# Moving the head that is scored alone ahead of the last pair, in a fused attention and GeGLU kernel

## The chip, the cores and the metric

The kernel runs on one core of one Trainium2 chip, in one launch. The metric is the device time of that launch in microseconds (us). Three runs of the kernel before took 1405.23, 1408.26 and 1406.68 us; their median is 1406.68 us.

## The reference, cut to what matters

One transformer block in float32: S = 2048 rows, D = 512, 32 query heads of 16 columns that share one key head and one value head, F = 1792.

```
q = layernorm(x) @ wq ; k = layernorm(x) @ wk ; v = layernorm(x) @ wv
h = x + softmax(q k^T / 4) v @ wo                     # 32 heads over one k and one v
h2 = h + (gelu(layernorm(h) @ w_gate) * (layernorm(h) @ w_up)) @ w_down
```

## The kernel before, in words

**Attention.** The 2048 query rows are four blocks of 512, the 32 heads eight groups of four, and the keys sixteen stretches of 128. One block, group and stretch is a *chunk*: 4 x 8 x 16 = 512 chunks, numbered here from 0 in the order of the work, so that chunk 128 begins the second block. For a chunk TensorE (PE) forms scores of two *pairs* of heads; a pair is two matmuls that run side by side in the upper and the lower 64 rows of the array (`scores`, L369 to L376, through `score_head`, L380). ScalarE (ACT) takes the exponential of a pair at once, 128x1024 (L376), into a tile `p`. Four matmuls then *weigh* the values with the four heads of the chunk (`weigh`, L386), summing in the PSUM bank `acc` over the sixteen chunks of a group; after the last of them VectorE (DVE) copies the sums out (`evacuate`, the copy `oT<-acc` at L399), and SyncE's queue (SP) sends them to memory and fetches them back turned. Two PSUM buffers of two banks hold the scores of a pair (`pss`), so a pair's scores wait for the exponential of the pair two before it.

**Dense products.** The output projection (`pp`), the gate and up projections (`pg`, `pu`) and the down projection (`pd`) of an earlier block are woven into the attention of the next. Each weight is split in a high and a low part, so a product is a list of terms. A product's upper 64 rows of the contraction are its *first* row and its lower 64 rows its *second*; `step` issues one matmul of a first row and one of a second row, six steps behind (`LAG`), and the two run side by side. Three PSUM banks serve these rows in turn (`take_bank`, from the front of the list `spare`); a bank is put back when its row has ended, and the next row in it waits for DVE's copy or add out of it (L623 and L626 for `pp`, L698 and L702 for `pg` and `pu`, L765 for `pd`). Other DVE work of a product stands in the list `later`, two entries of which `side(2)` issues at each row's end and at each cycle's start.

**The order of the work** is written out by hand. From pair 280 the main loop runs in cycles: `finish(RUN)` weighs four chunks in one run, then a string of moves is played, in which `s` scores a pair, `d` is a step, `2` and `1` score one head alone. A head alone fills one half of the array and a row of a dense product the other. `1` scores the second head of the next pair at the very end of a cycle, into a dense bank, and `2` its first head at the start of the next; so the strings are `2` + WOVEN after a cycle that ended with such a half, and FRESH after one that did not. ACT takes each of the two halves apart (128x512, L1089). A cycle in which the queue of dense products has too little ready is a PAUSE: single chunks, weighed and scored with no step. Pauses stand at chunks 244 to 247 and 372 to 379.

In what follows a *slot* is one place in PE's order that two matmuls share: a pair's two heads, a first and a second row, or half a pair and one row. A woven cycle is a run of four chunks and 26 slots: eight for scores (seven pairs, and the two halves) and eighteen for dense products, counting those beside the halves.

**The opening** of the dense work is the stretch from chunk 134 to chunk 152: the lead-in ends with six pairs in a row, five chunks are weighed in one run, and the four projections `pp_0_0` to `pp_0_3` of the first block follow. Each ends in a layer norm on DVE and GpSimd (POOL), and PE turns its result with four transposes (`pxt`, L636, `turn`), which DVE splits into `x2h` and `x2l` (L641, L642); `pg` starts when the last of the four is split. In the later blocks three of the four turns are DVE transposes of 32x32 blocks instead (`xt<-xb`, L657, `turn_blocks`).

A tanh (ACT, L714) is issued at a cycle's start (`bend`); its products on DVE (`gate`: L720, L723, then L732, L736) were put into `later` after the run of weighings had been issued.

Of the kernel before, what the change touches and what calls it, by code (L numbers as in the profile page):

```python
# [13 lines left out]
AF = mybir.ActivationFunctionType  # L14
# [41 lines left out]

AHEAD = {240: 3, 248: 2}

BOUND_CYCLES = (6, 8)

HOLD = -4

# [3 lines left out]
def kernel(  # L66
# [97 lines left out]
    def run(outer, first):  # L164
# [204 lines left out]
        def scores(i, p, qg, kc, u):  # L369

            third = width == 1 and (2 * i + u) % 3 == 2
            pool, tag, bufs = (ps, "s3", 1) if third else (pss, "s", 2)
            s = pool.tile([P, 2, T], F32, tag=tag, bufs=bufs, name=f"s_{i}_{u}")
            for a in range(2):
                score_head(s[:, a, :], qg, kc, u, a)
            nc.scalar.activation(p[:, 2 * u : 2 * u + 2, :], s, AF.Exp, scale=SCALE)  # L376

        def score_head(s, qg, kc, u, a):
            rows = slice(64 * a, 64 * a + KR)
            nc.tensor.matmul(  # L380
                s, kaug[rows, kc * P : (kc + 1) * P], qg[rows, u, :], start=True, stop=True
            )
# [201 lines left out]
        def side(n):  # L584
            while later and n > 0:
                later.pop(0)()
                n -= 1
# [468 lines left out]
        def open_pair(n):  # L1056

            nonlocal acc
            i, u = divmod(n, 2)
            b, r = divmod(i, PER)  # L1060
            g, kc = divmod(r, KC)
            if u == 0:
                if kc == 0:
                    cur["qg"] = qgs.pop((b, g))
                    acc = psa.tile([P, T], F32, tag="acc", bufs=1, name=f"acc_{b}_{g}")
                if kc == 2 and b * NG + g + 1 < NB * NG:
                    key = divmod(b * NG + g + 1, NG)
                    qgs[key] = load_q(*key)
                cur["p"] = sb.tile([P, 4, T], F32, tag="p", bufs=PB, name=f"p_{i}")
            return i, u, b, g, kc  # L1070

        def score(n):
            i, u, b, g, kc = open_pair(n)
            scores(i, cur["p"], cur["qg"], kc, u)
            if u == 1:
                pend.append((b, g, kc, cur["p"], acc, n))

        def score_half(n, a):
            if a == 1:
                cur["open"] = open_pair(n)  # L1080
            i, u, b, g, kc = cur["open"]
# [6 lines left out]
            score_head(s, cur["qg"], kc, u, a)  # L1088
            nc.scalar.activation(cur["p"][:, 2 * u + a, :], s, AF.Exp, scale=SCALE)  # L1089

        banks.close()
        psa = outer.enter_context(
# [6 lines left out]
        width = 1  # L1099


        n, lead = 0, 2 * PER + 24
        with tc.manual_schedule(engines={mybir.EngineType.SP, mybir.EngineType.DVE}):
            parts = None
            if first:
                work = later_q()
                parts = part_weights(early.enter_context(tc.tile_pool(name="parts", bufs=1)))


            normed = True  # L1110
# [12 lines left out]
            def norm():  # L1123
                nonlocal normed
                if not normed:
                    next(work)
                    normed = True

            def pace():
                nonlocal n, parts, db, tiny  # L1130
                if n == 2 * PER:
                    drain()
                    for _ in parts or ():
                        pass
# [12 lines left out]
                if n == 2 * PER + 8:  # L1147
                    prime()

            moves = {"s": pace, "p": visit, "n": norm, "v": partial(finish, 1)}  # L1150
            for move in OPENING + PERIOD * (PER // KC):
                moves[move]()
            while n < lead:
                pace()
                if n > lead - 6:
                    finish(len(pend) - RUN)
                elif n % 4 == 2 and len(pend) > 2:
                    finish(1)
                elif n % 4 == 0:
                    finish(len(pend) - 2)  # L1160
# [34 lines left out]
        def urgent():  # L1195
            i = at - 1 if left[0] else at
            return i < len(queue) and queue[i][0].startswith("pp") and any(
                queue[j][0].startswith("pg") for j in range(i, min(i + TB + 1, len(queue)))
            )

        def turns_left():
            return scaled_at and all(
# [1 line left out]
                for b, _ in scaled_at  # L1204
            )

        odd, cycle = False, 0
        while pend:
            if first and cycle in BOUND_CYCLES:
                bound_flag(BOUND_CYCLES.index(cycle))  # L1210
            cycle += 1
            last = n >= end - 2 * RUN
            steps = WOVEN.count("d") + 1
            want = 12 if urgent() else steps * AHEAD.get(n % (2 * PER), 1)
            idle = n == end or available() < (want if n < end - 2 * PER // 8 else steps)
            if idle and (n == end or urgent()):
                while available():
                    step()
            if idle and not available() and (
                at == len(queue) or queue[at - 1][0].startswith("pp")  # L1220
            ):
# [5 lines left out]
            idle = idle and not behind and available() < want  # L1227
            finish(1 if idle else RUN)
            clock += 4 if idle else 4 * RUN
            if behind:  # L1230
                for b_t in list(scaled_at):
                    del scaled_at[b_t]
                    turn(*b_t)
            for key in bent:
                later.extend(gate(*key))
            side(2 * len(bent))
            if idle:
                moves = "2" * odd + PAUSE[odd:]
            else:
                part = not last and not scaled_at  # L1240
                moves = ("2" + WOVEN if odd else FRESH) + "d1"[part]
            for move in moves:
                if move == "d":
                    if available():
                        step()
                elif move == "v":
                    finish(1)
                    clock += 4
                elif move == "1":
                    if clock - freed.get(spare[0], -EMPTY) < EMPTY or not available():  # L1250
                        if available():
                            step()
                        odd = False
                    else:
                        score_half(n, 1)
                        step(second=False)
                        odd = True
                elif move == "2":
                    score_half(n, 0)
                    if ahead > LAG:  # L1260
                        step(first=False)
                    n, odd = n + 1, False
                elif n < end:
                    score(n)
                    n += 1
                    clock += 1
        assert not odd
        while available():
            step()
# [386 lines left out]
```

## Time and profile before

| what | value |
|---|---|
| median of three runs | 1406.68 us |
| the profiled execution | 1408.69 us |
| its span, first to last instruction | 1406.9 us |
| mean granted TensorE clock | 0.996 |
| PE busy | 1383.1 us (98%) |
| ACT busy | 1035.2 us (74%) |
| DVE busy | 657.5 us (47%) |

The profiled execution is 1.8 us longer than its span and 2.0 us longer than the median of the three runs. A busy PE is not a PE at its peak: matmuls overlap by the model of their ends, so small waits between them do not show as idle time. They show as spacing between the starts of matmuls, and as waits of PEld, the part of PE that loads weights ahead of a matmul.

### The profile page before, as it was taken

How to read it: one execution, taken by the hardware profiler on the slowest of the kernel's cores; microseconds unless marked ns; L12 is line 12 of the kernel's file. 1: busy time of each engine (PE TensorE's matmuls, PEld its weight loads, DVE VectorE, ACT ScalarE, POOL GpSimd, SP SyncE). 2: the span in 40 equal slices, each digit the busy share in tenths (PEclk: the TensorE clock that was granted, in tenths of full speed). 3: DMA queues.
4: the chain of work that ended last, by engine and by line, in shares of the span. 5: the costliest groups of instructions: out<-in, count | busy, mean ns of one | idle time of the engine just before them, and what ended most of it. 6: DMA issues, size and time to landing. Idle time of an engine off the chain costs nothing.

```text
span 1406.9 us, 25386 instructions
## 1 busy us (share of the span) xinstructions
PE 1383.1 (98%) x10406; PEld 758.4 (54%) x10406; DVE 657.5 (47%) x1097; ACT 1035.2 (74%) x1241; POOL 239.5 (17%) x346
## 2 busy tenths in 40 slices
PE   9999999999999999999999999999999999999998
PEld 7533333325555555545555555545555555558886
DVE  7413131313364453547364453537455353546665
ACT  8899999986687877877787777787778777772000
POOL 7576777621000000001000000001100000002000
PEclk9999999999999999999999999999999999999999
DMA  4566776753222423311432333311333332333552
GB/s 162 165 214 194 236 236 231 221 175 112 80 92 71 138 96 118 102 57 43 157 110 87 132 91 114 102 58 35 136 105 116 102 103 82 123 115 125 192 205 95
DMA packets 66784, 180.32 MB, mean 128 GB/s; under 512 B 9672, under 2 KB 9672, under 8 KB 66628
## 3 DMA queue, kind: packets, MB, share of 16 engines
q1 hardware_dynamic: 55324, 143.29, 31.0%
q0 software_dynamic: 10208, 35.26, 7.6%
q8 instruction: 84, 1.38, 0.4%
q14 instruction: 40, 0.33, 0.1%
q10 hardware_dynamic: 1128, 0.07, 0.1%
HBM read 130.87 MB, written 47.45 MB: 127 GB/s over the span
## 4 chain that ended last, share of the span: by engine, by line
PE 89%; ACT 5%; DVE 3%; DMA 2%; issue 1%; POOL 0%; SPq 0%; ACTq 0%; POOLq 0%
PE acc L386 32%; PE s L380 19%; PE pg L836 8%; PE pu L836 8%; PE pd L836 7%; ACT p L376 5%; PE pq L225 3%; PE pd L874 3%; PE pg L874 3%; PE pu L874 3%; PE pp L836 1%; PE pp L938 1%; DMA w<-w_d 1%; DMA x<-in_A_x_dram 1%; DVE xt L657 1%
## 5 line engine op out<-in xcount | busy, mean ns | idle before, releaser
L376 ACT ACTIVATE p<-s 128x1024 f32<-128x1024 f32 x940 | 878.5, 1050 | 40.7 <-PE s L380 37.9
L386 PE MATMUL acc<-p,v_sb 128*32 128x512 f32 x4096 | 481.9, 599 | 0.0
L380 PE MATMUL s<-qg,kaug 50*128 50x512 f32 x1984 | 421.5, 426 | 9.2 <-ACT p L376 7.3
L380 PEld LDWEIGHTS s<-qg,kaug 50*128 50x128 f32 x1984 | 184.7, 184 | 272.4 <-ACT p L376 141.3
L386 PEld LDWEIGHTS acc<-p,v_sb 128*32 128x32 f32 x4096 | 113.1, 109 | 253.2 <-issue 241.4
L1089 ACT ACTIVATE p<-s 128x512 f32<-128x512 f32 x168 | 106.0, 631 | 190.7 <-PE s L380 150.8
L836 PE MATMUL pg<-x2h,w 64*128 64x512 f32 x672 | 209.7, 401 | 1.4 <-DVE g L702 0.7
L836 PE MATMUL pu<-x2h,w 64*128 64x512 f32 x672 | 208.4, 398 | 0.4 <-DMA w<-w_d 0.4
L836 PE MATMUL pd<-w,gh 64*128 64x512 f32 x624 | 115.5, 394 | 1.9 <-DVE gh L732 1.1
L143 POOL TENSOR_SCALAR rstd<-mv 128x1 f32<-128x1 f32 x16 | 3.6, 223 | 668.2 <-DVE mv L141 668.0
L836 PEld LDWEIGHTS pg<-x2h,w 64*128 64x128 f32 x672 | 99.1, 187 | 10.7 <-DVE g L702 2.1
L765 DVE TENSOR_TENSOR h<-h,pd 128x512 f32<-128x512 f32 x80 | 54.9, 686 | 104.5 <-PE pd L836 79.8
L836 PEld LDWEIGHTS pu<-x2h,w 64*128 64x128 f32 x672 | 97.7, 186 | 7.2 <-issue 0.7
L836 PE MATMUL pg<-x2l,w 64*128 64x512 f32 x336 | 101.3, 395 | 0.2 <-DVE x2l L642 0.2
L836 PE MATMUL pu<-x2l,w 64*128 64x512 f32 x336 | 99.9, 392 | 0.0
L399 DVE COPY oT<-acc 128x512 f32<-128x512 f32 x32 | 22.1, 691 | 146.0 <-PE acc L386 145.8
L836 PE MATMUL pd<-w,gl 64*128 64x512 f32 x312 | 81.1, 400 | 0.0
L836 PEld LDWEIGHTS pd<-w,gh 64*128 64x128 f32 x624 | 69.7, 187 | 11.5 <-DVE gh L732 1.5
L992 ACT ACTIVATE ga<-ga 128x512 f32<-128x512 f32 x14 | 8.8, 632 | 88.5 <-DVE ga L989 88.5
L702 DVE TENSOR_TENSOR u<-u,pu 128x512 f32<-128x512 f32 x42 | 28.8, 685 | 85.2 <-PE pu L836 56.4
L422 DVE RECIPROCAL oc<-oc 128x128 f32<-128x128 f32 x64 | 56.6, 920 | 17.7 <-DMA oc<-acc_d 13.8
L702 DVE TENSOR_TENSOR g<-g,pg 128x512 f32<-128x512 f32 x42 | 28.8, 687 | 67.7 <-PE pg L836 52.2
(256 smaller groups left out, 1538.6 us busy)
## 6 DMA issues: line engine op xcount, KB each, us to landing
w<-w_d SPq DMA_DIRECT2D x126, 512.0 KB
w<-w_d SPq DMA_DIRECT2D x21, 1024.0 KB
qg<-q_d SPq DMA_DIRECT2D x62, 200.0 KB
q_d<-qh SPq DMA_DIRECT2D x32, 256.0 KB
acc_d<-oT SPq DMA_DIRECT2D x31, 256.0 KB
oc<-acc_d SPq DMA_DIRECT2D x124, 64.0 KB
w_d<-w_0b POOLq DMA_DIRECT2D x14, 512.0 KB, 4.2
w_d<-w_1b POOLq DMA_DIRECT2D x14, 512.0 KB, 3.8
```

The source lines that it names most:

```text
L225: nc.tensor.matmul(pq, wt[c][:, d, :], xt[:, d, :], start=(n == 0), stop=(n == 3 * DC - 1),)
L376: nc.scalar.activation(p[:, 2 * u : 2 * u + 2, :], s, AF.Exp, scale=SCALE)
L380: nc.tensor.matmul(s, kaug[rows, kc * P : (kc + 1) * P], qg[rows, u, :], start=True, stop=True)
L386: nc.tensor.matmul(acc[32 * j : 32 * j + 32, :], v_sb[:, kc, :], p[:, j, :], start=(kc == 0), stop=(kc == KC - 1), skip_group_check=True,)
L399: nc.vector.tensor_copy(oT, acc)
L422: nc.vector.reciprocal(oc[:, 1, sl], oc[:, 1, sl])
L657: nc.vector.transpose(raw[32 * k : 32 * k + 32, :, 32 * i : 32 * i + 32], x[32 * i : 32 * i + 32, :, k, :],)
L702: nc.vector.tensor_tensor(half, half, bank, op=ALU.add)
L765: nc.vector.tensor_tensor(hs[b, t], hs[b, t], bank, op=ALU.add)
L836: nc.tensor.matmul(bank, lhsT[r], rhs[r], start=(k == 0), stop=(k == n - 1), skip_group_check=True,)
L874: nc.tensor.matmul(bank, lhsT, rhs, start=(i == 0), stop=(i == len(ts) - 1))
L1089: nc.scalar.activation(cur["p"][:, 2 * u + a, :], s, AF.Exp, scale=SCALE)
```

## The change

Four things change; the diff below is cut to them.

- `1` moves from behind the last `s` to before it, in WOVEN and FRESH: the lone head of pair n+1 is scored before pair n, and its exponential is issued to ACT before that of pair n. `open_pair` now hands over all that belongs to a pair, so that pair n+1 can be opened before pair n is scored. EMPTY, the age in ticks that a dense bank must have before a lone head may use it, goes from 6 to 5, and the move now stands one tick earlier. No lone head is scored while a projection `pp` is among the last two products begun (`projecting`).
- The opening gets lists of its own (CYCLES): twice, cycles that weigh three, three and two chunks. Where the queue has too little ready, a list's plain string weighs and scores single chunks. The lead-in ends one pair earlier (279).
- A run of four weighs three chunks, then issues the first two of a waiting tanh's products to DVE, and only then weighs the fourth, behind which the copy of the sums is issued.
- The rule for when a cycle pauses is rewritten: `urgent` is gone, and the reserve (RESERVE) holds for all blocks but the last.

```diff
+CYCLES = (
+    (3, "ssdddddsdddsddds", "vssvssvs"),
+    (3, "ssdddddsdddsddds", "vssvssvs"),
+    (2, "ssdddddsdddsdddsddds", "ssvssvss"),
+)
+OPENING_LISTS = 2
-WOVEN = "sdddsdddsdddsdddsdddsdds"
-FRESH = "ssdddddsdddsdddsdddsddsds"
+WOVEN = "2sdddsdddsdddsdddsdddsdd1s"
+FRESH = "ssdddddsdddsdddsdddsddds1s"
-EMPTY = 6
-AHEAD = {240: 3, 248: 2}
-BOUND_CYCLES = (6, 8)
+EMPTY = 5
+RESERVE = {240: 3, 248: 2}
+BOUND_CYCLES = (2, 4)
...
-        n, lead = 0, 2 * PER + 24
+        n, lead = 0, 2 * PER + 23
...
+        for i in range(OPENING_LISTS):
+            for j, (count, woven, plain) in enumerate(CYCLES):
+                idle = available() < woven.count("d")
...
+                bent = before(idle)
+                if not idle:
+                    finish(count)
...
+        def projecting():
+            return any(name.startswith("pp") for name, *_ in queue[max(at - 2, 0) : at])
...
-            want = 12 if urgent() else steps * AHEAD.get(n % (2 * PER), 1)
-            idle = n == end or available() < (want if n < end - 2 * PER // 8 else steps)
+            if n < end - 2 * PER:
+                steps *= RESERVE.get(n % (2 * PER), 1)
+            idle = n == end or available() < steps
...
-            finish(1 if idle else RUN)
+            finish(1 if idle else RUN - 1)
             clock += 4 if idle else 4 * RUN
+            for key in bent:
+                later.extend(gate(*key))
+            side(2 * len(bent))
+            if not idle:
+                finish(1)
...
                 elif move == "1":
-                    if clock - freed.get(spare[0], -EMPTY) < EMPTY or not available():
+                    if (
+                        last or scaled_at or projecting() or not available()
+                        or clock - freed.get(spare[0], -EMPTY) < EMPTY
+                    ):
                         if available():
                             step()
                     else:
-                        score_half(n, 1)
+                        whole, half = open_pair(n), open_pair(n + 1)
+                        score_half(half, 1)
                         step(second=False)
```

**PE, the end of a woven cycle.** The rows are those before the run that weighs chunks 332 to 335 (in the profile, the run that starts at 818.10 us). `s_335_1` is the cycle's last pair, `s_336_0_1` the lone head, `pu` and `pg` the dense rows. Before:

```order
L380 MATMUL s_335_0_8728<-qg_2_4_7961,kaug_70 128x512 x2
L836 MATMUL pu_1_8_0_8720<-x2h_1_6753,w1_1_8_1_8602 128x512
L836 MATMUL pg_1_8_1_8697<-x2h_1_6753,w1_1_8_0_8553 128x512
L836 MATMUL pu_1_8_0_8720<-x2l_1_6754,w1_1_8_1_8602 128x512
L836 MATMUL pg_1_8_1_8697<-x2l_1_6754,w1_1_8_0_8553 128x512
L380 MATMUL s_335_1_8736<-qg_2_4_7961,kaug_70 128x512 x2
L380 MATMUL s_336_0_1_8742<-qg_2_5_8379,kaug_70 128x512
L836 MATMUL pu_1_8_0_8720<-x2h_1_6753,w1_1_8_1_8602 128x512
L386 MATMUL acc_2_4_8311<-p_332_8631,v_sb_71 32x512 x4
```

With the change:

```order
L388 MATMUL s_335_0_8716<-qg_2_4_7949,kaug_70 128x512 x2
L844 MATMUL pu_1_8_0_8708<-x2h_1_6714,w1_1_8_1_8590 128x512
L844 MATMUL pg_1_8_1_8685<-x2h_1_6714,w1_1_8_0_8541 128x512
L844 MATMUL pu_1_8_0_8708<-x2l_1_6715,w1_1_8_1_8590 128x512
L844 MATMUL pg_1_8_1_8685<-x2l_1_6715,w1_1_8_0_8541 128x512
L388 MATMUL s_336_0_1_8726<-qg_2_5_8367,kaug_70 128x512
L844 MATMUL pu_1_8_0_8708<-x2h_1_6714,w1_1_8_1_8590 128x512
L388 MATMUL s_335_1_8730<-qg_2_4_7949,kaug_70 128x512 x2
L394 MATMUL acc_2_4_8295<-p_332_8615,v_sb_71 32x512 x4
```

The lone head with its dense row has moved ahead of the last pair, which now has three slots between it and the pair before it, as every other pair of the cycle has.

**PE, the end of the opening.** `pxt_0_1` to `pxt_0_3` are the transposes of the second to the fourth row of the block, `acc` the weighings, `pg_0_0` the first gate product. Before:

```order
L636 MATMUL pxt_0_1_3718<-ident_60,xb_0_1_3263 128x128 x4
L636 MATMUL pxt_0_2_3727<-ident_60,xb_0_2_3267 128x128 x4
L386 MATMUL acc_1_1_3474<-p_148_3599,v_sb_71 32x512 x4
L386 MATMUL acc_1_1_3474<-p_149_3646,v_sb_71 32x512 x4
L386 MATMUL acc_1_1_3474<-p_150_3677,v_sb_71 32x512 x4
L386 MATMUL acc_1_1_3474<-p_151_3694,v_sb_71 32x512 x4
L636 MATMUL pxt_0_3_3752<-ident_60,xb_0_3_3613 128x128 x4
L380 MATMUL s_152_0_3762<-qg_1_1_3236,kaug_70 128x512 x2
L380 MATMUL s_152_1_3766<-qg_1_1_3236,kaug_70 128x512 x2
L836 MATMUL pg_0_0_0_3770<-x2h_0_3257,w1_0_0_0_3261 128x512
```

With the change:

```order
L644 MATMUL pxt_0_1_3692<-ident_60,xb_0_1_3263 128x128 x4
L644 MATMUL pxt_0_2_3701<-ident_60,xb_0_2_3267 128x128 x4
L394 MATMUL acc_1_1_3502<-p_147_3592,v_sb_71 32x512 x4
L388 MATMUL s_150_0_3715<-qg_1_1_3236,kaug_70 128x512 x2
L388 MATMUL s_150_1_3719<-qg_1_1_3236,kaug_70 128x512 x2
L394 MATMUL acc_1_1_3502<-p_148_3622,v_sb_71 32x512 x4
L388 MATMUL s_151_0_3728<-qg_1_1_3236,kaug_70 128x512 x2
L388 MATMUL s_151_1_3732<-qg_1_1_3236,kaug_70 128x512 x2
L394 MATMUL acc_1_1_3502<-p_149_3658,v_sb_71 32x512 x4
L388 MATMUL s_152_0_3741<-qg_1_1_3236,kaug_70 128x512 x2
L644 MATMUL pxt_0_3_3745<-ident_60,xb_0_3_3604 128x128 x4
L388 MATMUL s_152_1_3754<-qg_1_1_3236,kaug_70 128x512 x2
```

Chunks 147 to 151 are now weighed one by one with pairs between them and no dense step, and the fourth transpose stands in the midst of them; `pg` follows only after the run that weighs chunks 152 to 155 and the two pairs behind it. The pause of four chunks at 244 to 247 is no longer there, and both orders have the same dense products issued by chunk 248, but for one matmul (954 before, 953 now).

**DVE, the projections of the second block.** `h_1_1<-pp_1_1_0` is the add that empties the bank of the first row of projection `pp_1_1`; `xt<-xb` are the 32x32 transposes, `oc` and `o_hi` the work on the attention's output. Before:

```order
L612 TENSOR_SCALAR xb_1_0_3725<-h_1_0_6685,mv_2_1_0_6747,rstd_2_1_0_6750 128x512
L623 TENSOR_TENSOR h_1_1_6778<-pp_1_1_0_6688,xb_1_1_3734 128x512
L657 STREAM_TRANSPOSE xt_1_0_6755<-xb_1_0_3725 32x4x32 x8
L626 TENSOR_TENSOR h_1_1_6778<-h_1_1_6778,pp_1_1_1_6762 128x512
L140 BN_STATS st_2_1_1_6812<-h_1_1_6778 128x6
```

With the change:

```order
L620 TENSOR_SCALAR xb_1_0_3699<-h_1_0_6681,mv_2_1_0_6708,rstd_2_1_0_6711 128x512
L430 RECIPROCAL oc_1_3_6075<-oc_1_3_6075 128x128
L447 TENSOR_TENSOR oc_1_3_6075<-oc_1_3_6075 128x128
L141 CAST o_hi_1_4325<-oc_1_3_6075 128x128
L142 TENSOR_TENSOR o_lo_1_4326<-oc_1_3_6075,o_hi_1_4325 128x128
L430 RECIPROCAL oc_1_3_6075<-oc_1_3_6075 128x128
L447 TENSOR_TENSOR oc_1_3_6075<-oc_1_3_6075 128x128
L141 CAST o_hi_1_4325<-oc_1_3_6075 128x128
L142 TENSOR_TENSOR o_lo_1_4326<-oc_1_3_6075,o_hi_1_4325 128x128
L665 STREAM_TRANSPOSE xt_1_0_6716<-xb_1_0_3699 32x4x32 x16
L631 TENSOR_TENSOR h_1_1_6792<-pp_1_1_0_6684,xb_1_1_3708 128x512
```

Two quarters of the output's division, which stood ahead of these rows before, and all sixteen transposes now stand between the layer norm's last step and the add that empties the bank. The second row of `pp_1_2` is the next to use that bank.

More of the change, by code (lines that the diff above doesn't have):

```diff
@@ L1069, in open_pair, with score, score_half @@
                 cur["p"] = sb.tile([P, 4, T], F32, tag="p", bufs=PB, name=f"p_{i}")
[L1070 to L1074, printed above, removed]
+            return i, u, cur["p"], cur["qg"], (b, g, kc, cur["p"], acc, n)
+        def score(n, opened=None):
+            i, u, p, qg, chunk = opened or open_pair(n)
+            scores(i, p, qg, chunk[2], u)
             if u == 1:
[L1076 to L1081, printed above, removed]
+                pend.append(chunk)
+        def score_half(opened, a):
+            i, u, p, qg, chunk = opened
             assert u == 0
@@ L1154, in run @@
                 pace()
[L1155 to L1157 removed]
+                if n % 4 == 2 and len(pend) > 2 and n < lead - 1:
                     finish(1)
@@ L1205, in turns_left @@
             )
-        odd, cycle = False, 0
+        half, whole, cycle = None, None, 0
         while pend:
@@ L1226, in run @@
             behind = idle and n < end and turns_left()
-            idle = idle and not behind and available() < want
-            finish(1 if idle else RUN)
+            idle = idle and not behind and available() < steps
+            finish(1 if idle else RUN - 1)
             clock += 4 if idle else 4 * RUN
+            for key in bent:
+                later.extend(gate(*key))
+            side(2 * len(bent))
+            if not idle:
+                finish(1)
             if behind:
@@ L1233, in run @@
                     turn(*b_t)
-            for key in bent:
-                later.extend(gate(*key))
-            side(2 * len(bent))
             if idle:
-                moves = "2" * odd + PAUSE[odd:]
+                moves = PAUSE if half is None else "2" + PAUSE[1:]
             else:
-                part = not last and not scaled_at
-                moves = ("2" + WOVEN if odd else FRESH) + "d1"[part]
+                moves = FRESH if half is None else WOVEN
             for move in moves:
```

43 lines of the change are left out of this document (23 added, 20 removed).

## The prediction, made before the changed kernel was run

> **What bounds the kernel now.** I read the span by stages first, cut where chunks 134, 152, 244, 248, 280, 380 and 408 begin to be weighed.
>
> ```profile
> 305.39:362.51 57.12, 51.70 (x364) 26.71 (x363) 22.66 (x37) 36.93 (x42) 3.85 (x9) 0.94 0.40 139
> 362.51:592.74 230.23, 230.23 (x1935) 127.33 (x1933) 113.90 (x174) 178.77 (x220) 0.00 (x0) 1.00 0.33 105
> 592.74:600.76 8.02, 7.33 (x50) 2.10 (x48) 3.21 (x6) 7.77 (x11) 0.00 (x0) 1.00 0.06 23
> 600.76:686.76 86.00, 82.36 (x678) 46.16 (x676) 48.76 (x109) 61.17 (x71) 8.81 (x14) 1.00 0.21 67
> 686.76:919.12 232.36, 231.24 (x1934) 128.75 (x1932) 113.22 (x175) 180.01 (x221) 0.00 (x0) 1.00 0.35 113
> 935.19:1007.82 72.63, 71.70 (x594) 39.11 (x593) 43.61 (x100) 52.72 (x62) 8.86 (x14) 1.00 0.14 46
> 1007.82:1247.92 240.10, 240.10 (x2018) 134.53 (x2016) 118.06 (x180) 186.65 (x230) 2.25 (x4) 1.00 0.36 117
> ```
>
> The columns are the stage, its length, and busy time of PE, PEld, DVE, ACT and POOL, then the granted clock. The second and the last row are woven cycles only: 23 and 24 of them, 10.01 and 10.00 us each, PE never idle. The work is the same after the change, so what can be won is spacing between matmuls. PEld's waits say where it is, PE's own where a dense bank is late:
>
> ```profile
> PEld s L380 <- ACT p L376: 147.9, 344, 1.0
> ```
>
> ```profile
> PE s L380 <- DVE h L626: 1.8, 2, 1.2
> ```
>
> The first is 148 us in 344 waits, most of them harmless, since PEld runs ahead of PE. The end of one woven cycle shows the one that is not: PE, then PEld, then ACT.
>
> ```profile
> 816.93 0.40 PE L836 MATMUL pg<-x2h,w 64*128 64x512 f32 x1
> 817.17 0.39 PE L836 MATMUL pu<-x2l,w 64*128 64x512 f32 x1
> 817.44 0.50 PE L380 MATMUL s<-qg,kaug 50*128 50x512 f32 x2
> 817.78 0.40 PE L836 MATMUL pu<-x2h,w 64*128 64x512 f32 x1
> 818.10 0.64 PE L386 MATMUL acc<-p,v_sb 128*32 128x512 f32 x4
> ```
>
> ```profile
> 817.44 0.19 PEld L380 LDWEIGHTS s<-qg,kaug 50*128 50x128 f32 x2 [0.31 <-ACT p L376]
> ```
>
> ```profile
> 812.70 6.52 ACT L376 ACTIVATE p<-s 128x1024 f32<-128x1024 f32 x7
> ```
>
> A slot is 0.235 us (816.93 to 817.17). The last pair's load waits for ACT, so the two slots from 817.17 to 817.78 take 0.61 us instead of 0.47: **0.14 us per woven cycle**. ACT takes a pair every 0.91 us, PE offers one every four slots (0.94 us); only the last pair, after three, comes too soon.
>
> **The change, part by part.**
>
> *The lone head ahead of the last pair.* It fills the slot in which the last pair waited. No instruction is added; ACT takes the half first, so the last exponential ends about 0.5 us later, near 819.7. The fourth chunk of the run that begins at 818.10, 3 x 0.89 us later at 820.8, is the first to need it. So 0.14 us goes, bounds 0 and 0.14, and a cycle is 9.87 us. What is late next is nothing within 0.1 us: that pair's load is free at 817.44, its new place is 817.64. EMPTY and the move shift together by one tick; banks made scores wait twice only, both during projections.
>
> A fresh cycle, one without a half in front, is held by ACT to its eighth pair, then plays one slot more:
>
> ```profile
> 610.60 0.50 PE L380 MATMUL s<-qg,kaug 50*128 50x512 f32 x2 [0.17 <-ACT p L376]
> 610.93 0.40 PE L836 MATMUL pd<-w,gl 64*128 64x512 f32 x2
> 611.26 0.64 PE L386 MATMUL acc<-p,v_sb 128*32 128x512 f32 x4
> ```
>
> ```profile
> 600.83 3.57 PE acc L386 x32
> 611.33 3.57 PE acc L386 x32
> 623.13 3.57 PE acc L386 x32
> ```
>
> The chain's runs are 10.50 us apart. With the last slot moved under the wait, 10.50 - 0.23 = **10.27 us**. The next cycle took 11.80: 1.3 us more, where `pd` waits for `gh`. In the new order the add of `pd_0_8_1` still stands ahead of `gh`, so that stays.
>
> *Products ahead of the sums' copy.* Where a group ends and a tanh is due, the chain goes over DVE:
>
> ```profile
> 818.17 3.62 PE acc L386 x32
> 821.81 0.69 DVE oT L399
> 823.13 0.69 DVE ga L723
> 823.83 0.61 DVE g L702
> 824.48 0.49 PE pg L836
> 828.56 0.55 PE acc L386
> ```
>
> From run to run this cycle takes 10.39 us, not 10.00. With both `ga` steps (some 1.3 us) ahead of the copy, in time in which DVE waits for the sums, `g` ends before PE asks. Four such cycles stand in the second block: 4 x 0.39 = 1.6 us.
>
> *The opening.* Its end was a chain over DVE, and its start ran at half clock:
>
> ```profile
> 335.90 0.63 PE pxt L636 x4
> 347.71 0.70 DVE h L626
> 354.91 0.92 PE pg L836 x2
> ```
>
> ```profile
> 307.50:310.91 3.41, 1.95 (x12) 0.77 (x12) 3.31 (x6) 3.41 (x5) 0.00 (x0) 1.00 0.99 297
> 310.91:314.33 3.42, 3.42 (x22) 0.80 (x24) 0.67 (x1) 2.25 (x3) 0.00 (x0) 0.50 1.03 409
> ```
>
> In the 7.2 us from 347.71 to 354.91, PE had one run (3.57 us) and little else to do; now five single chunks stand there. And six pairs in a row left PE busy for 1.95 of 3.41 us, whereupon 3.42 us ran at a clock of 0.50, for a loss of 1.7 us. The new lead-in has five pairs, with a weighing between the second and the third, so I take that loss as gone. New sum, chunk 134 to 156, a cycle being 0.89 us per chunk (3.57 / 4), 0.235 per slot and 0.2 at the ends (9.87 - 3.57 - 26 x 0.235): five pairs at ACT's pace 4.6; two cycles of three chunks and 16 slots, 6.6 each; one of two chunks and 20 slots with a turn (0.6), 7.3; one of three chunks and 23 slots with two turns and a short wait, 9.9; five single chunks with twelve pairs at 0.91 and the ends, 11.3; a fresh cycle, 10.3. That is 56.6. With 23 woven cycles (226.9), chunk 248 comes 283.5 us after chunk 134; before it took 57.12 + 230.23 + 8.02 = 295.4. **Gain 11.9**, the pause at 244 to 247 having moved to where PE waited anyway.
>
> *The projections of the second block.* Here the new DVE order costs. Durations are from the third block's projections:
>
> ```profile
> 954.18 0.94 DVE L422 RECIPROCAL oc<-oc 128x128 f32<-128x128 f32 x1
> 955.96 0.94 DVE L422 RECIPROCAL oc<-oc 128x128 f32<-128x128 f32 x1
> 963.58 0.69 DVE L626 TENSOR_TENSOR h<-h,pp 128x512 f32<-128x512 f32 x1 [1.18 <-PE pp L836]
> 966.67 0.68 DVE L623 TENSOR_TENSOR h<-pp,xb 128x512 f32<-128x512 f32 x1
> 967.27 5.04 DVE L657 STREAM_TRANSPOSE xt<-xb 32x128 f32<-32x128 f32 x16
> ```
>
> From the add that ends `pp_1_0` to the end of the norm is 3.1 us, two quarters of the division 2 x 1.78, sixteen transposes 5.0, the add that frees `pp_1_1`'s bank 0.7: 12.4 us, from about 0.45 us after the last matmul of `pp_1_0`. The second row of `pp_1_2`, which needs that bank, stands 13 steps behind it: one run (3.57), 17 slots (4.0) and ends, 8.6 us. PE waits 12.4 + 0.45 - 8.6 = 4.2 us, in the cycle of chunk 260; some 0.3 come back, ACT having caught up. A wait that long leaves PE less busy than the 1.95 of 3.41 us above, so I add 1.7 us for a second of half clock: 10.27 + 3.9 + 1.7 = 15.9. Stage 600.76 to 686.76: woven 9.87, 11.57, 10.27, 15.9, 10.27, 10.87 (one turn), 10.27, 9.87 = 88.9 against 86.00, **a loss of 2.9**. In the third block the same sixteen transposes stand behind that add, as before.
>
> *The rest.* 686.76 to 919.12: 23 woven cycles, 226.9, and 0.5 of the 0.8 us that the stage has beyond 23 x 10.00 and the 1.6 above, which I leave in: gain 5.0. 935.19 to 1007.82: five fresh cycles, one fresh with a turn, one woven, 72.1: gain 0.5. The last 24 woven cycles: 236.9, gain 3.2. The last slot before the tail: 0.2. The tail is unchanged, and RESERVE and BOUND_CYCLES add no instruction: the one sets where pauses stand, which the order shows, the other moves two small DVE steps.
>
> **Sum:** 11.9 - 2.9 + 5.0 + 0.5 + 3.2 + 0.2 = 17.9 us. The profiled execution's 1408.69 us becomes 1390.8; it lies 2.0 above the median, so the forecast is 1406.68 - 17.9 = **1388.8 us**.
>
> **The rivals.**
>
> *The wait only moves (0.12).* If the last pair finds ACT no further on, since ACT's 0.91 us per pair leaves 0.03 per four slots, 72 woven cycles keep 0.14 us: 10.1 us back, 1398.9. Against it: pairs two to six of the cycle above lose nothing at that spacing.
>
> *The opening keeps its waits (0.10).* If the turns wait for DVE at the end of the last three-chunk cycle, or the clock falls in the single chunks, the 8.5 us that are not woven cycles go: 1397.3. Against it: the single chunks of 592.74 to 600.76 ran at a clock of 1.00.
>
> *The projections cost less (0.15).* If that bank comes in time, 5.6 us return: 1383.2. Against it stands DVE's order.
>
> *The clock stays full at chunk 260 (a third of the forecast's 0.60).* If PE's wait falls so that neither window of 3.41 us around it is as empty as the one at 307.50, 1.7 us return: 1387.1, inside the forecast's own range. [...]
>
> *Slower (0.03).* In the first block SP's queue now meets the end of a group before a weight load:
>
> ```profile
> 376.94 0.32 SPq L451 DMA_DIRECT2D acc_d<-oT  x1
> 380.81 0.37 SPq L541 DMA_DIRECT2D w<-w_d  x1
> ```
>
> The load waits 3.9 us behind the sums. It is issued three products ahead, 36 steps or two cycles of 9.87 us, so PE waits for it only where it takes more than the 15.8 us left to land; 3.5 us of that at each of six group ends, 21 us, would make 1409.8.
>
> **How the numbers follow.** My forecast has 0.60. Its own range, from the unknown 1.7 us at 260 and some 3 us on the opening, is 1384 to 1393; the opening's rival takes it up to 1397.5 and the cheaper projections down to 1382; the wait that only moves, at 1398.9, and the slower case are left out, 0.15 together. Three runs of the kernel spread by 0.2%, about what a measurement can tell from no change (2.8 us): faster 0.93, same 0.04, slower 0.03.
>
> **What would show it.** Right: woven runs 9.87 us apart; no 10.39; no half clock near 311 and 355, but one near chunk 262; PE waiting some 4 us there for DVE `h`. Wrong: woven runs still 10.00 apart, or `pg` waiting for `x2l` in the opening, or waits of PE for `w`.

## The result, and the profile after

| | before | after |
|---|---|---|
| median, four runs each on one chip | 1407.47 us | 1394.35 us |
| lowest to highest | 1405.23 to 1410.2 us | 1393.4 to 1396.19 us |
| ratio, 95% interval | | 0.9908 [0.9886, 0.9929] |
| the profiled execution | 1408.69 us | 1393.4 us |
| its span | 1406.9 us | 1391.6 us |
| mean granted TensorE clock | 0.996 | 0.998 |

The change makes the kernel 13.1 us faster by the medians and 15.3 us by the spans of the profiled executions. 1388.8 us was forecast, 17.9 us below before. The measured median lies 1.35 us above the range that the forecast set for itself (1384 to 1393 us) and inside the wider one, 1382 to 1397.5 us, that took in the opening's rival; the sum was 2.6 us too high against the spans.

The span of after by stages, cut at the same chunks as before, but for the first two, whose border is chunk 156 (362.99), where woven cycles begin. The columns are the stage, its length, busy time of PE, PEld, DVE, ACT and POOL, the granted clock, and DMA.

```profile
305.59:362.99 57.40, 55.31 (x413) 27.16 (x411) 22.86 (x37) 44.03 (x48) 3.85 (x9) 1.00 0.40 140
362.99:590.22 227.23, 227.23 (x1935) 130.17 (x1933) 112.78 (x174) 178.87 (x220) 0.00 (x0) 1.00 0.33 106
590.22:679.33 89.11, 83.61 (x679) 46.11 (x677) 52.04 (x115) 61.12 (x69) 8.87 (x14) 0.98 0.20 66
679.33:907.20 227.87, 227.52 (x1934) 130.74 (x1932) 113.54 (x175) 179.37 (x221) 0.00 (x0) 1.00 0.35 115
907.20:923.82 16.62, 14.99 (x99) 4.24 (x97) 3.20 (x6) 15.57 (x19) 0.00 (x0) 1.00 0.10 32
923.82:995.94 72.12, 71.62 (x595) 39.51 (x593) 44.01 (x101) 52.20 (x58) 8.86 (x14) 1.00 0.14 46
995.94:1232.79 236.85, 236.85 (x2018) 135.46 (x2016) 117.71 (x180) 186.75 (x230) 2.28 (x4) 1.00 0.36 118
```

The second and the last row are 23 and 24 woven cycles: 9.88 and 9.87 us each. Against the working:

| chunks | before | forecast | after |
|---|---|---|---|
| 134 to 248 | 295.4 | 283.5 | 284.6 |
| 248 to 280 | 86.0 | 88.9 | 89.1 |
| 280 to 372 | 232.4 | 227.4 | 227.9 |
| 372 to 380 (the pause) | 16.1 | 16.1 | 16.6 |
| 380 to 408 | 72.6 | 72.1 | 72.1 |
| 408 to 504 | 240.1 | 236.9 | 236.9 |

The end of the woven cycle before chunk 332, PE and then PEld, the same place as in the prediction:

```profile
817.48 0.40 PE L844 MATMUL pg<-x2l,w 64*128 64x512 f32 x2
817.71 0.39 PE L388 MATMUL s<-qg,kaug 50*128 50x512 f32 x1
817.72 0.39 PE L844 MATMUL pg<-x2h,w 64*128 64x512 f32 x1
817.94 0.41 PE L388 MATMUL s<-qg,kaug 50*128 50x512 f32 x2
818.27 0.64 PE L394 MATMUL acc<-p,v_sb 128*32 128x512 f32 x4
```

```profile
817.74 0.19 PEld L388 LDWEIGHTS s<-qg,kaug 50*128 50x128 f32 x2
```

The lone head (817.71) now stands ahead of the last pair (817.94), 0.23 us apart, and the pair's load at 817.74 has no wait for ACT in brackets. The two largest waits of PE, after (total, times, longest):

```profile
PE s L388 <- ACT p L384: 5.0, 14, 0.7
PE pp L844 <- DVE h L631: 3.9, 1, 3.9
```

The second is the wait that the prediction put into the projections of the second block. Behind it the clock falls, as forecast, in windows of 3.41 us:

```profile
631.43:634.84 3.41, 0.90 (x8) 0.77 (x10) 3.17 (x9) 0.00 (x0) 1.38 (x2) 1.00 0.18 28
634.84:638.25 3.41, 3.41 (x21) 1.77 (x21) 2.37 (x6) 2.61 (x3) 1.31 (x3) 0.50 0.13 49
```

### The profile page after: what moved, and what is told of

Read it like the earlier page. It is cut to its first block, busy times and chain, and to the rows that moved or that the text cites. A ratio compares the mean times of both kernels' runs of the same rounds, so it can differ in the third digit from the quotient of the medians.

```text
span 1391.6 us, 25347 instructions
## 1 busy us (share of the span) xinstructions
PE 1370.5 (98%) x10406; PEld 762.6 (55%) x10406; DVE 656.1 (47%) x1097; ACT 1033.9 (74%) x1231; POOL 241.8 (17%) x346
## 4 chain that ended last, share of the span: by engine, by line
PE 90%; ACT 5%; DVE 2%; DMA 2%; issue 1%; POOL 0%; SPq 0%; ACTq 0%; POOLq 0%; DVEq 0%
PE acc L394 32%; PE s L388 20%; PE pu L844 8%; PE pg L844 7%; PE pd L844 7%; ACT p L384 5%; PE pq L233 3%; PE pd L882 3%; PE pg L882 3%; PE pu L882 3%; PE pp L844 2%; PE pp L946 1%; DMA w<-w_d 1%; PE pd_rest L894 1%; PE pk L1426 1%
## 5 line engine op out<-in xcount | busy, mean ns | idle before, releaser
L384 ACT ACTIVATE p<-s 128x1024 f32<-128x1024 f32 x950 | 900.3, 1051 | 64.7 <-PE s L388 61.0
L388 PE MATMUL s<-qg,kaug 50*128 50x512 f32 x1984 | 408.3, 419 | 6.1 <-ACT p L384 5.0
L844 PE MATMUL pg<-x2h,w 64*128 64x512 f32 x672 | 206.8, 398 | 0.0
L1095 ACT ACTIVATE p<-s 128x512 f32<-128x512 f32 x148 | 92.7, 626 | 152.8 <-PE s L388 90.9
L728 DVE SCALAR_TENSOR_TENSOR ga<-ga,g 128x512 f32<-128x512 f32 x42 | 28.8, 686 | 77.5 <-ACT ga L722 77.4
L430 DVE RECIPROCAL oc<-oc 128x128 f32<-128x128 f32 x64 | 56.6, 921 | 17.9 <-DMA oc<-acc_d 14.0
```

The costliest lines, as they stand in the source:

```text
L388: nc.tensor.matmul(s, kaug[rows, kc * P : (kc + 1) * P], qg[rows, u, :], start=True, stop=True)
L430: nc.vector.reciprocal(oc[:, 1, sl], oc[:, 1, sl])
L728: nc.vector.scalar_tensor_tensor(a, a, 1.0, g, op0=ALU.add, op1=ALU.mult)
L844: nc.tensor.matmul(bank, lhsT[r], rhs[r], start=(k == 0), stop=(k == n - 1), skip_group_check=True,)
L1095: nc.scalar.activation(p[:, 2 * u + a, :], s, AF.Exp, scale=SCALE)
```

## The experiments

Cycle times below are read as the distance between the starts of two runs of weighings in the chain of waits. The ratios of medians are each against the kernel before on the same chip. Line numbers of a kernel that differs by a few lines are its own.

**The head put back (head_last).**

```diff
-WOVEN = "2sdddsdddsdddsdddsdddsdd1s"
-FRESH = "ssdddddsdddsdddsdddsddds1s"
-EMPTY = 5
+WOVEN = "2sdddsdddsdddsdddsdddsdds1"
+FRESH = "ssdddddsdddsdddsdddsddsds1"
+EMPTY = 6
...
-                        whole, half = open_pair(n), open_pair(n + 1)
+                        half = open_pair(n)
```

> The changed kernel with the lone head put back behind the run's last pair (and the bank rule at six ticks again), all else kept. Theory (the head's place alone is worth the 0.12 us of a woven cycle and the slot of a fresh one): woven cycles go from 9.88 back to 10.00 us, 71 x 0.12 = 8.7 us; fresh cycles in the projections from 10.27 to 10.50, nine of them 2.1 us; the pause of chunks 372 to 379 from 16.62 back to 16.07, -0.55; 10.3 us slower than the changed kernel, near 1404.6. Rival (the shorter cycles come from the gate products and the split run, not from the head): woven cycles stay at 9.88, no change.

Measured: 1406.87 us, ratio 0.9993 [0.9984, 1.0003]. Three runs of weighings of this kernel, from its chain, and PEld just ahead of the second:

```profile
816.30 3.58 PE acc L394 x32
...
826.30 3.57 PE acc L394 x32
...
836.31 3.57 PE acc L394 x32
```

```profile
825.57 0.19 PEld L388 LDWEIGHTS s<-qg,kaug 50*128 50x128 f32 x2 [0.29 <-ACT p L384]
```

The cycles are 10.00 and 10.01 us again, and the last pair's load waits for ACT again. From chunk 134 to 508 this kernel takes 13.5 us more than after: 9.5 in 72 woven cycles, 2.8 in twelve fresh ones, 2.2 in the cycles of chunks 260 and 264 (a wait for DVE of 4.5 us and two windows of half clock), less 0.6 in the pause and 0.3 in the cycle of chunk 280. Without the head's new place, all the rest of the change is worth nothing that can be measured.

**The head alone, on the kernel before (head_alone).** The same move in the strings of before, with the pairs opened as in after; nothing else.

```diff
-WOVEN = "sdddsdddsdddsdddsdddsdds"
-FRESH = "ssdddddsdddsdddsdddsddsds"
-EMPTY = 6
+WOVEN = "sdddsdddsdddsdddsdddsdd"
+FRESH = "ssdddddsdddsdddsdddsddds"
+EMPTY = 5
...
-                moves = ("2" + WOVEN if odd else FRESH) + "d1"[part]
+                moves = ("2" + WOVEN if odd else FRESH) + ("1s" if part else "ds")
```

> The kernel before with the lone head ahead of the run's last pair, and its bank rule at five ticks, as the only change: opening, order of the gate products and counts of steps as before. Theory: 71 woven cycles of 0.12 us, 8.5 us, and a slot in each of some five fresh cycles, 1.2 us, less 0.55 us in the pause of chunks 372 to 379: 9.2 us faster than the kernel before, so that all other parts of the change together are worth only some 4 to 6 us. Rival (the head needs the new lists around it: at the old order of the gate products the earlier exponentials make other waits): 3 us faster or less.

Measured: 1398.3 us, ratio 0.993 [0.9914, 0.9947], 10.1 us faster than before. So the head's place is most of the gain by itself. Its opening (chunks 134 to 152), 23 woven cycles and the pause at chunk 244:

```profile
306.96:359.46 52.50, 48.27 (x364) 26.22 (x362) 20.17 (x35) 36.54 (x42) 3.85 (x9) 1.00 0.38 140
359.46:586.69 227.23, 227.23 (x1935) 130.59 (x1933) 113.34 (x174) 178.92 (x220) 0.00 (x0) 1.00 0.33 106
586.69:594.84 8.15, 7.69 (x50) 2.11 (x48) 3.25 (x6) 7.82 (x11) 0.00 (x0) 1.00 0.08 31
```

The old opening is here too, with its six pairs in a row, and it ran at a clock of 1.00. From chunk 134 to 248 that is 287.9 us; after takes 284.6. So what after has beyond the head is worth 3.2 us there at the same clock. Two named waits go with it: `pxt` waits 0.3 us, not 0.8, and `pg` no longer waits for `x2h` and `x2l`, 0.9 us in head_alone. The stretch holds the lists, the missing pause and the products' new place together, and no run takes the lists or the pause rule alone.

**The products put back behind the copy (gates_after).** TensorE's order is that of after.

```diff
-            finish(1 if idle else RUN - 1)
+            finish(1 if idle else RUN)
...
-            if not idle:
-                finish(1)
```

> The changed kernel with the gate products put back behind the copy of the sums; TensorE's order is the same. Theory: the four cycles of chunks 284, 300, 332 and 364 wait for g again and take 10.27 us (9.88 + 0.39) to 10.39, 1.6 to 2.0 us slower; all others unchanged. Rival (since the lone head moved, g is in time without it): those four stay at 9.87, no change.

Measured: 1401.08 us, ratio 0.9958 [0.9941, 0.9974]: slower than after by far more than expected. The four cycles take 10.63 us, not 10.27 to 10.39, and five cycles of the first dense block that were not expected to change take more as well: those of chunks 172, 204 and 236 10.63, those of 188 and 220 10.31. The nine cycles together take 6.2 us more, and the stretch from chunk 134 to 508 6.3. The spans are 7.9 us apart; 1.2 us of the rest lies ahead of chunk 134, where a window of half clock at 286.68 came before anything that the edit touches. The chain through the cycle of chunk 284:

```profile
697.70 0.69 DVE oT L407
698.39 0.61 DVE ga L728
...
699.02 0.69 DVE ga L731
699.71 0.60 DVE g L710
...
703.30 0.61 DVE u L710
703.91 0.04 issue
703.95 0.49 PE s L388
```

and, in after, DVE at the same place:

```profile
692.03 0.69 DVE L728 SCALAR_TENSOR_TENSOR ga<-ga,g 128x512 f32<-128x512 f32 x1 [4.14 <-ACT ga L722]
692.76 0.69 DVE L731 TENSOR_TENSOR ga<-ga,u 128x512 f32<-128x512 f32 x1
693.52 0.69 DVE L407 COPY oT<-acc 128x512 f32<-128x512 f32 x1
694.13 0.68 DVE L710 TENSOR_TENSOR g<-g,pg 128x512 f32<-128x512 f32 x1
```

Two things are late behind the copy: `g`, as in before, and at the cycle's end the lone head, whose dense bank `u` frees only at 703.91. Before, the head came a slot later and the cycle took 10.39; head_alone, with the head moved and the products behind the copy, has the 10.63 too, and head_last, with the products ahead and the head behind, has 10.00. So the two parts of the change lean on each other: the earlier head makes the products' new place worth 0.76 us at such a cycle, not 0.39. The five cycles of the first dense block are another matter: head_alone, which keeps the old opening, does not have them (its 23 woven cycles from chunk 152 take 227.23 us). They came where the earlier head, the new opening and the old place of the products met; no run has the new opening and the old place with the head behind. With the products behind the copy, chunk 134 to 248 took 288.1 us, no less than head_alone's 287.9: the 3.2 us above hang on the products too.

**The transposes and the add (no_blocks, two_blocks).** The prediction's one loss was the cycle of chunk 260. In both, DVE's order alone differs from after's; 2 in place of 0 leaves eight of the sixteen transposes ahead of the add.

```diff
         def before(idle):
+            took = bool(outs)
...
-            side(100 if idle else 2)
+            side(0 if took and b_pp() else 100 if idle else 2)
...
+        def b_pp():
+            return 0 < at < len(queue) and queue[at][0].startswith("pp_1")
```

> The changed kernel with one edit: at the cycle of chunk 260 the sixteen transposes of the first tile no longer stand ahead of the add that frees the bank of pp_1_1's first row; TensorE's order is the same. Theory (the 3.90 us wait of pp for DVE h, and the 3.41 us of half clock from 634.84, both come from those 5.04 us of DVE): the add ends 5.04 us earlier, before PE asks; no wait of pp for h, no half clock there, the cycle of chunk 260 takes 10.3 us and not 15.40, the next 10.3 and not 10.68, 5.5 us less in all, a span near 1386.1. Rival 1 (the wait moves: the transposes now stand between the later adds, and pp_1_3 or the fill-in products wait instead): the cycles of chunks 260 to 276 keep a wait of 1 to 4 us at another tile, 1.5 to 4 us less in all. Rival 2 (the clock falls there for a reason other than the wait): the wait goes but 3.41 us at 0.50 stay, 3.8 us less.

> The changed kernel with eight of the sixteen transposes ahead of that add, eight behind it. Theory: 2.5 us of DVE's 5.04 go, so the wait of pp for h is 3.90 - 2.5 = 1.4 us. Under the view that the clock falls after a window of 3.41 us in which PE was busy for less than about 2, a wait of 1.4 us leaves PE 2 us or more busy in every window: no half clock, 4.1 us less than the changed kernel. If the clock falls all the same (windows with PE busy 2.52 of 3.42 us had a half clock behind them in the opening of the kernel before): 2.4 us less. If the wait isn't made of these transposes at all: no change.

Measured: no_blocks 1388.18 us, ratio 0.9868 [0.9851, 0.9884]; two_blocks 1390.29 us, 0.9885 [0.9868, 0.9901]. The chain of after at that place, the last transpose, the add and the product:

```profile
632.86 0.31 DVE xt L665
633.16 0.03 issue
633.20 0.70 DVE h L631
633.90 0.04 issue
633.94 0.50 PE pp L844
```

DVE of no_blocks, where the add follows the division at once:

```profile
627.91 0.29 DVE L142 TENSOR_TENSOR o_lo<-oc,o_hi 128x128 fp32r<-128x128 f32 x1
628.12 0.68 DVE L631 TENSOR_TENSOR h<-pp,xb 128x512 f32<-128x512 f32 x1
628.72 2.49 DVE L665 STREAM_TRANSPOSE xt<-xb 32x128 f32<-32x128 f32 x8
```

and PE's wait in two_blocks:

```profile
PE pp L844 <- DVE h L631: 1.3, 1, 1.3
```

With 16, 8 and 0 transposes ahead of the add, the wait is 3.9, 1.3 and 0 us, and the cycles of chunks 260 and 264 together take 26.1, 22.2 and 20.5; only the first has a half clock in it. The step from 8 to 0 is 1.7, of which PE's wait is 1.3; that from 16 to 8 is 3.9, of which 2.6 are the wait, and the other 1.3 go together with the half clock. Elsewhere the largest difference is 0.5 us in chunks 280 to 372. Run again on another chip (no_blocks_again), with this expectation:

> The run no_blocks once more, on the chip of the run beside it. Theory: 0.987 of the kernel before, its cycle of chunk 260 at 10.27 us and no half clock behind it. Rival (its first time was helped by windows that lay well): a half clock in or behind the cycles of chunks 256 to 264, and a ratio nearer to 0.991.

it gave 1388.83 us, 0.9866 [0.9847, 0.9885], the cycle 10.27 again, and its only half clock before the end at 285.54, ahead of the opening. The loss that the prediction read from DVE's order was real, and a change to that order alone takes it away: 5.6 us in the two cycles, some 6 in all beyond the change.

**Three steps of the pair ahead of the copy, then all four (gh_first, pairs_first).** Both on top of no_blocks; the first line added is that of gh_first, the other two are those of pairs_first.

```diff
-            side(2 * len(bent))
+            side(3 * len(bent))
...
+            adding = 0 < at < len(queue) and queue[at][0].startswith("pd")
+            side((4 if adding else 2) * len(bent))
```

> The kernel with the transposes behind the add (run no_blocks) and one edit more: of a bent half, the step that makes gh goes ahead of the copy of the sums too, three steps in place of two. In the cycle of chunk 252 ga is ready at 603.28, the copy starts at 603.80, gh only at 606.76, behind the copy and an add that waits 1.66 us for pd; PE waits 1.12 us. Theory: gh (0.42 us) fits into the 0.52 us in which DVE waits for the sums, PE's wait for gh goes, the cycle of chunk 252 falls from 11.57 to 10.3 us, 1.2 us less than no_blocks, a span near 1384.2. Rival: elsewhere the step of 0.42 us comes ahead of adds that free banks, and cycles with a tanh grow by 0.1 to 0.4 us each: no gain, or some us slower than no_blocks.

> The kernel with the transposes behind the add (run no_blocks), and both gh and gl ahead of the copy of the sums, but only where the next product is pd. In gh_first the cycle of chunk 252 fell only from 11.57 to 11.11 us: with gh made early, gl (0.61 us) still stood behind the add of pd that starts at 606.19. Theory: with gl ahead as well nothing of the pair is late, the wait of pd goes, that cycle takes 10.3 us, 1.3 us less than no_blocks beside it, a median near 1386.9. Rival: the copy of the sums, 0.6 us later, or the adds of g and u behind the two steps elsewhere make other waits of 0.1 to 0.8 us at the ends of groups: no gain.

Measured: 1387.91 us, 0.9853 [0.9837, 0.9869], and 1388.31 us, 0.9866 [0.9849, 0.9884]. The chain of gh_first in the cycle of chunk 252:

```profile
606.19 0.69 DVE h L773
606.88 0.61 DVE gl L744
607.49 0.04 issue
607.54 0.96 PE pd L844 x6
```

Now `gl` was what came last: the cycle fell to 11.11, a miss. With `gl` ahead too (pairs_first) it took 10.31, and no wait of `pd` was left. The two cycles of chunks 188 and 220, where the same steps come ahead of other adds, grew by 0.16 us each. By medians neither kernel can be told from no_blocks, so the 1.3 us are shown in the cycle, not in the time.

**Pairs in a row (pairs_in_row).** One weighing of the lead-in moved; the first list weighs as before.

```diff
-                if n % 4 == 2 and len(pend) > 2 and n < lead - 1:
+                if n % 4 == 2 and len(pend) > 2 and n < lead - 5:
```

> The changed kernel with one weighing of the lead-in moved: chunk 135 is weighed in the run behind the five pairs, not between the second and the third of them, so that five pairs stand in a row; all else kept. Theory of the prediction (a row of pairs leaves PE emptier than about 2 of 3.41 us, and the clock falls): 0.9 us for the weighing that loses its cover, and 3.41 us at 0.50 behind it, 1.7 us: 2.6 us slower than the changed kernel by its span. Rival 1 (five pairs are short enough, or the windows lie otherwise): 0.9 us slower, clock 1.00 all through the opening. Rival 2 (ACT alone sets the time there): no change.

The edit was not what this says: it moved the weighing of chunk 134, not 135, so that four pairs stood in a row and not five. (The run also lets the first list weigh five chunks; only three wait there, and three are weighed.) Measured: 1395.05 us, 0.9902 [0.9885, 0.9918], beside 1395.45 us for after on that chip. From chunk 133 to 136 it took 6.38 us, after 6.42. ACT was busy for 6.19 of the 6.38: it sets the time there, as rival 2 had it. A window of half clock at 298.86 lay ahead of the four pairs. The run says nothing on rows of six.

**The same programs again (after_again, before_again, before_third).**

> The changed kernel once more, on the chip of these runs, to see which stretches of half clock return. Theory (the 3.90 us wait at chunk 260 empties a window of 3.41 us wherever the windows lie): a half clock begins between 633 and 638 again, the cycle of chunk 260 takes 14.5 to 15.9 us. Rival (the windows run free of the kernel and lay badly by chance): no half clock there, 13.7 to 14 us for that cycle.

> The kernel before once more, for the clock in its opening. Theory of the prediction (six pairs in a row empty a window, and the clock falls behind it): half clock near 311 again, and near 355. Rival (the windows run free of the kernel, and its opening falls into half clock in some executions only): full clock at one of the two places or at both, and the cycle of chunk 135 at 11.3 us in place of 13.04, or that of chunk 148 at 12.2 in place of 13.89.

> A third execution of the kernel before, as the run beside it: under the theory half clock near 311 and near 355 in both, under the rival in neither or in one of them.

after_again: 1395.45 us, 0.9907 [0.9891, 0.9924]. The wait is 3.9 us again, and behind it two windows of half clock, not one, from 631.94; the cycle of chunk 260 takes 16.13 us, 0.2 above what was expected:

```profile
628.52:631.94 3.42, 1.36 (x11) 0.72 (x7) 3.27 (x12) 2.13 (x3) 0.00 (x0) 1.00 0.00 0
631.94:635.35 3.41, 1.57 (x8) 1.27 (x10) 3.17 (x8) 0.00 (x0) 1.89 (x2) 0.50 0.30 77
635.35:638.76 3.41, 3.41 (x17) 1.72 (x17) 2.17 (x7) 2.55 (x3) 0.79 (x2) 0.50 0.00 0
```

before_again, 1408.48 us, has the half clock at 311.77 and at 356.14, as before had it at 310.91 and near 355. before_third, 1407.69 us, has none near 311, one at 347.68 (and one at 286.24, ahead of the opening, as head_alone has at 286.82); chunk 134 to 248 took 293.2 us there, in the other two 295.3 and 295.4. Its window where before's was emptied, and the two around its half clock:

```profile
310.13:313.54 3.41, 2.44 (x18) 0.97 (x22) 3.24 (x5) 3.41 (x5) 0.00 (x0) 1.00 0.98 339
344.26:347.68 3.42, 2.65 (x14) 1.51 (x12) 1.14 (x2) 3.29 (x4) 0.69 (x2) 1.00 0.00 0
347.68:351.09 3.41, 3.41 (x16) 1.81 (x20) 2.34 (x5) 0.00 (x0) 1.45 (x3) 0.50 0.38 96
```

The old opening thus has two windows of half clock in two executions, one in a third, and none in head_alone. Of the ten profiled executions with the new lists none has one between 305 and 360 us. Six pairs in a row do not bring a half clock by themselves: it came in some executions of the old opening and not in others.

## Why the prediction was right, and where its sum was off

**The lone head: right, and shown.** 0.13 us in a woven cycle (10.01 to 9.88, and 10.00 to 9.87) against the 0.14 that was read from the trace, undone by head_last and reproduced by head_alone. Plain fresh cycles came at 10.26 to 10.29, forecast 10.27. The rival in which the wait only moves would have left the cycles at 10.00. (The margin was thinner than the working had it: ACT's row of seven pairs in 6.52 us is 0.93 us per pair, not 0.91, against PE's 0.94.)

**The pause at chunks 372 to 379: a term missed, 0.55 us.** I held it unchanged. With the head ahead, the last exponential of the cycle before ends 3.36 us into the pause, not 3.04, and the next begins at 3.82, not 3.25: 16.62 us against 16.07, and 16.05 in head_last.

**The products: right at their place, too small in their reason.** The four cycles take 9.85 to 9.88 us, as forecast. But I priced them at the old 0.39 us; beside the new head and opening the same order is worth 6.2 us, five cycles of the first dense block included. The sum held by luck: it took each part's worth from the trace of before, and the new order prevented losses that I had not seen.

**The opening: right in size, mixed in its cause.** 11.9 was forecast, 10.7 came. The single chunks took 12.0 us, not 11.3, and the cycle of two chunks 7.66, not 7.3, where PE waited 0.3 us for the sums to come back from memory (`pxt<-DMA oc`); the cycle with two turns was 0.4 shorter. Of the 10.7, what after has beyond the head is worth 3.2 at an equal clock; the other 7.5 are the head (3.0 in 23 woven cycles, and its share in the opening's own) and before's two windows of half clock. The words "six pairs in a row left PE busy for 1.95 of 3.41 us, whereupon 3.42 us ran at a clock of 0.50" are where the working took one execution's half clock for a fixed cost of that order. (Its 226.9 us for 23 cycles of 9.87 are 227.0.)

**The projections of the second block: right step by step.** A wait of 4.2 us was worked out, 3.90 came, and a half clock behind it; the 8.6 us set against DVE's chain hold 1.0 us of "ends" that the working does not derive, so the close fit is in part luck; the cycle was forecast at 15.9 and took 15.40 and 16.13 in two executions. no_blocks and two_blocks show both causes.

**What is left of the difference.** The spans fell by 15.3 us and the sum gave 17.9: 1.2 in the opening, 0.55 in the pause, 0.5 in chunks 280 to 372 (0.2 of it in the cycle of chunk 280, which took between 10.18 and 11.71 us in the runs, the longest where `pu` waits 1.4 or 1.5 us for its weights), 0.2 in chunks 248 to 280 and 0.2 ahead of chunk 134. The other 3.0 us between 1388.8 and 1394.35 are the profiled executions: before's lay 2.0 above its median, as the prediction said, and after's 0.95 below its own.

## What to carry to other kernels

A wait of a tenth of a microsecond that stands in every cycle is worth more than a long one that stands once: some seventy moves of one matmul brought 10 us, and a rewritten opening 3, and those only with the products' new place beside it. When a part of a change looks small by the trace of before, ask what it is worth beside the other parts: the products' order was worth 1.6 us by the old cycles and 6.2 beside the other parts. And a list of small tasks that is emptied "while there is nothing to do" can stand in front of the one step that frees a bank; eight transposes cost 1.7 us there, sixteen 5.6.

## What the runs showed of the hardware

The half clock is not a function of the program. Chunk for chunk the same program ahead of the opening had PE busy for 2.28 of 3.41 us from 283.27 in both of these executions; gates_after first, then after:

```profile
283.27:286.68 3.41, 2.28 (x16) 0.72 (x14) 0.00 (x0) 3.41 (x5) 2.44 (x3) 1.00 0.52 169
286.68:290.10 3.42, 3.42 (x16) 0.88 (x18) 0.00 (x0) 2.87 (x4) 2.30 (x3) 0.50 0.38 156
```

```profile
283.27:286.68 3.41, 2.28 (x16) 0.65 (x14) 0.00 (x0) 3.34 (x4) 2.84 (x5) 1.00 0.74 234
286.68:290.10 3.42, 3.42 (x30) 1.27 (x26) 0.00 (x0) 3.29 (x5) 2.75 (x4) 1.00 0.38 155
```

One fell to 0.50 and one did not. The two half clocks of before, from 310.91 and 355.29, last 3.41 us each and begin 44.4 us apart, 13 times that; the windows of this page are the stretches of 3.41 us that these two fit into. Of other windows at full clock, the clock fell behind those in which PE was busy for 0.90 us (after, from 631.43), 1.36 (after_again, 628.52), 1.95 and 2.52 (before, 307.50 and 351.87) and 2.65 (before_third, 344.26), and not behind those with 1.71 (before_third, 334.02), 1.95 (head_alone, 634.98), 2.03 (after, 628.01), 2.44 (before_third, 310.13) and 2.57 us (head_alone, 307.30). In before and after, between 30 and 1370 us, it fell behind none in which PE was busy for more than 2.52. The windows do not lie at one place of the kernel: in two executions of the kernel before, the half clock in the opening began 5.5 us behind the first weighing of chunk 134 in one (305.39 to 310.91) and 6.1 us in the other (305.69 to 311.77); and the wait of 3.9 us left PE idle for 1.4 and 2.5 us of two windows in after, for 2.1 and 1.8 us of two in after_again. What decides between 1.7 and 2.65 us stays open. Behind that wait of 3.9 us the clock fell in both of these executions, for one window in after and for two in after_again, and behind one of 4.5 us in head_last for two; behind the 1.3 us of two_blocks, in a window with PE busy for 2.07 us (from 629.05), it stayed at 1.00. For a prediction on this kernel it means that a stretch which leaves PE busy for 1.7 to 2.65 us of a window is to be priced at a share of 1.7 us (an estimate: half of a window of 3.41, at the measured clock of 0.50), not at the whole.
